# A re-planned instruction order, and GpSimd as a third engine for the attention's exponentials, in a four-layer transformer chain

## The chip, the cores and the metric

The kernel runs on one core of one Trainium2 chip. The metric is device time in microseconds of one execution. Times are medians of several runs; the profile is one further execution.

## The reference, cut to what matters

One sequence of 2048 tokens, width 1024, 32 heads of 32. Four residual layers alternate: A (linear attention with a learned softmax feature map), B (softmax attention), A, B, with the same weights each time they recur.

```python
def _A_ref(x, wqkv, w_phi, wo):            # q, k, v per head from x @ wqkv
    pq = jnp.einsum("bhsd,hdf->bhsf", q, w_phi)
    phi_q = jnp.concatenate([_softmax(pq), _softmax(-pq)], axis=-1)   # phi_k the same way
    kv = jnp.einsum("bhsf,bhsd->bhfd", phi_k, v)
    z  = jnp.einsum("bhsf->bhf", phi_k)
    o = einsum("bhqf,bhfd->bhqd", phi_q, kv) / (einsum("bhqf,bhf->bhq", phi_q, z)[..., None] + 1e-6)
    return o.transpose(0, 2, 1, 3).reshape(B, S, D) @ wo
def _B_ref(x, wqkv, wo):
    scores = jnp.einsum("bhqd,bhkd->bhqk", q, k) * (Dh ** -0.5)
    o = jnp.einsum("bhqk,bhkd->bhqd", _softmax(scores), v)
    return o.transpose(0, 2, 1, 3).reshape(B, S, D) @ wo
x = x + _A_ref(_layernorm(x), ...); x = x + _B_ref(_layernorm(x), ...)   # twice
```

Inputs and output are bf16.

## The kernel before

The kernel does not leave its order to a scheduler of the framework. It builds a list of operations, each with an engine, an expected duration, dependencies, buffers and a due time (`prio`), and a planner written in the file (`Sched`) places them in one fixed order for each engine. `LAT` (what passes from the end of an operation to the start of one on another engine), `act_us`, `dve_us`, `MM4` and the literals beside each operation are its expected durations; `WINDOW`, `QUOTA`, `AHEAD`, `NEAR`, `KL`, `PH` and the other capitals set how far ahead work may be taken, how many buffers a kind may hold and when side work is due. Once it is emitted, every engine runs its instructions strictly in that order and waits on semaphores.

Each of the two turns (`layer` 0 and 1) has an A part and a B part. In the A part TensorE products dominate: keys and values (`a_keys`), queries (`a_queries`), the output product (`a_out`); then `ln_rows` normalises each chunk of 512 tokens for B. `LN_DVE` says whether the row sums of that normalisation are taken on VectorE (`bn_stats`, L580) or on ScalarE (two passes with an accumulator, L586 and L588).

The B part is `attention`. Its work is 2048 units a layer: one unit is one head, 128 keys and 512 queries, a score tile of 128x512 in PSUM. The exponential of the scores goes to two engines:

- `group` takes up to three units (`WIDE`), scores them on TensorE side by side in rows of the array (L1148) into one of two buffers of three PSUM banks, and ScalarE exponentiates them in one instruction (L1208; 128x1536, or 128x1024 where a group has two units).
- A spare unit from some `AHEAD` units later may ride with a group in the fourth row, or as the third of a two-unit group. VectorE takes it out of PSUM (`convert`, L1290) as an integer whose bits hold the power of two, and later builds the exponential from the bits (`exp_dve`) by bit operations (L1102, L1105, or L1111, L1114) and products of two SBUF tensors (L1098). Up to two such units form a pair. In the second layer (`SPLIT`) the value is a sum of two bf16 parts, which costs TensorE one more product. `EACH` says whether the two units of a pair are computed singly.

The queries are scaled beforehand so that a score is the exponent of two times 2^23 (`ONE`).

The products with the values and with ones (L1337, both in one slot of the array) read the exponentials from SBUF, in the order of the units. In PSUM bank 7 fillers take their turn: projections of keys, values and queries, output products, in the first layer also the next A part's keys and values, and, where TensorE would have worked too little in the last microseconds, products that compute nothing (`idle`, `idle_acc`, L544 with onesD, L1573). GpSimd (POOL) sets a few buffers to zero and casts reciprocals (L779); it does nothing in the second attention. All DMAs are issued on SP's queue.

Of the kernel before, what the change touches and what calls it, by code (L numbers as in the profile page):

```python
# [46 lines left out]
LAT = {"PE": 0.25, "ACT": 0.2, "DVE": 0.1, "POOL": 0.2, "SP": 2.0, "AQ": 2.0}  # L47
# [13 lines left out]
class Sched:  # L61
# [134 lines left out]
    def run(self):  # L196
# [27 lines left out]
        while left:  # L224
# [107 lines left out]
WINDOW = 80.0  # L332
SOON = {"slabk": 24.0, "wo": 16.0, "w2": 4.0}
RESERVE = 12 * 1024
LONG = {"kT", "v", "slab", "slabk", "xn", "xn1", "kvacc", "kvm", "zm", "wnat"}
MODEST = {"slabk", "xn1", "e1", "vp1", "pkf", "wo", "bo"}
QUOTA = {"pk": 3, "pv": 2, "kv": 1, "mm": 5, "cmp": 2, "bc": 4, "num": 1, "wt": 4, "wx": 2, "fil": 4,
         "e": 6, "vp": 6, "e1": 4, "vp1": 4, "E": 8, "q2": 2, "kt": 4, "w2": 5, "oT": 26, "T": 4, "den": 2,
         "eq": 8, "ns": 4, "cw": 6, "hl": 6, "oc": 2, "slab": 7, "slabk": 3, "fin": 4,
         "rs": 8, "pkf": 1, "cden": 2, "part": 8, "w2r": 1,  # L340
         "wo": 1, "st": 4, "xo": 8, "bn": 4, "xs": 1, "xy": 4, "xx": 1, "E1": 7}
CORE = {"E", "E1", "T", "den", "cden", "oT"}
E_SIZE = 3 * 1024
HOLES = 2
# [10 lines left out]
EACH = (False, False)  # L355
LAG = 8
KL = (19, 32)
KS = (3, 5.5)
VS = (5.0, 7.0)
WQ_AFTER = 2  # L360
BY_DVE = 2
LR = 18
LAG_X = 4
LN_DVE = (True, True)
LN_PE = (3, 3)
WO = 6
KD = 7
HALF = (False, True)
VH = 3.0
QL = (11, 12)  # L370
AW = 23
OUT_AT = (230, 248, 268)
GO = 2.6
BO = 295
PT = 2.0
QB = 13
PH = (1, 22, 44)
LA = 9
AHEAD_AT = 5
P0 = (133, 167, 240)  # L380
GAPS = (1.5, 1.25, 1.75)
PK = (152, 192, 262)
STEP = 2.5
AWAY = (-2, 12)
MIX = (lambda i: 5, lambda i: 2)
LOAD = (4.0, 2.5)
AHEAD = (36, 34)
SLACK = 10.0
NEAR = (26, 18)
LEAD = 3.0  # L390
MOST = (lambda i: 0 if i < 1 else 7, lambda i: 0 if i < 1 else 6 if i < 6 else 40)
# [6 lines left out]
def dve_us(n):  # L398
    return n / 960 + 0.15
# [5 lines left out]
BACKLOG = 1.0  # L405
KV_MM = 0.042
# [3 lines left out]
def kernel(  # L410
# [49 lines left out]
    zz = const.tile([P, 16], F32, tag="zz")  # L460

# [3 lines left out]
    nc.vector.memset(eps[:], EPS_LN)  # L465
    make_identity(nc, ident[:])
# [65 lines left out]
    def dma(prio, fn, deps=(), bufs=(), q="SP", kb=256, issue=0.55, bulk=False):  # L532
        o = op(q, issue, fn, deps, bufs, prio, lat=2.0 + kb / 200.0)
        o.size, o.bulk = 256 if kb == 600 else kb, bulk
        return o
# [11 lines left out]
    MM4 = 0.225  # L547
# [534 lines left out]
    def exp_dve(pair, prio, each):  # L1082
# [6 lines left out]
        for lo, hi in [(k, k + 1) for k in range(n)] if each else [(0, n)]:  # L1089
# [4 lines left out]
            def ts(fn, deps, bufs):  # L1094
                return sch.later("DVE", w * 512 / 1920 + 0.15, fn, deps, bufs, prio)

            def stt(out_, in0, scalar, in1, dep, bufs):
                return sch.later("DVE", dve_us(w * 512), lambda: nc.vector.scalar_tensor_tensor(  # L1098
                    out=out_(), in0=in0(), scalar=scalar, in1=in1(), op0=ALU.add, op1=ALU.mult), [dep], bufs, prio)
            got = done[-1:] + pair["got"][lo:hi]  # L1100
            if pair["split"]:
                m = ts(lambda y_v=y_v, x_v=x_v: nc.vector.tensor_scalar(  # L1102
                    out=x_v().bitcast(I32), in0=y_v().bitcast(I32), scalar1=0x007FFFFF, scalar2=0x3F000000,
                    op0=ALU.bitwise_and, op1=ALU.bitwise_or), got, [y_b, x_b])
                a = ts(lambda y_v=y_v, e2_v=e2_v: nc.vector.tensor_scalar(  # L1105
                    out=e2_v().bitcast(U16), in0=high(y_v()), scalar1=0x7F80, scalar2=EXP2S_D,
                    op0=ALU.bitwise_and, op1=ALU.bitwise_or), [m], [y_b, e_b])
                h = stt(x_v, x_v, EXP2S_B, x_v, a, [x_b])
                done.append(stt(e_v, x_v, EXP2S_C, y_v, h, [x_b, y_b, e_b]))
                continue  # L1110
            m = ts(lambda y_v=y_v, x_v=x_v: nc.vector.tensor_scalar(  # L1111
                out=x_v().bitcast(I32), in0=y_v().bitcast(I32), scalar1=0x007FFFFF, scalar2=0x3F800000,
                op0=ALU.bitwise_and, op1=ALU.bitwise_or), got, [y_b, x_b])
# [5 lines left out]
            done.append(stt(e_v, x_v, EXP2_C, y_v, h, [x_b, y_b, e_b]))  # L1119
        return done  # L1120

    def attention(base, kT, vT, q_of, gate, most, mix, turns, pos, split, ahead, near, load, each):
# [7 lines left out]
        av_of, e_of, taken = {}, {}, set()  # L1130
# [22 lines left out]
        def holds(u):  # L1153
            return (kT[u[1]][0], q_of[(u[0], u[1])][0])
# [11 lines left out]
        def group(make):  # L1166
# [38 lines left out]
            so = make("PE", 0.24, sfn, sum((needs(u) for u in grp), []), [s_b], prio - 2, "r", n >= 2, [s_b])  # L1205
# [47 lines left out]

        def spare(rows, turn, more):

            pair = state["pair"]
# [26 lines left out]
        def convert(so, u, s_b, s_v, turn):  # L1283

            pair = state["pair"]
# [4 lines left out]
            pair["got"].append(sch.later("DVE", dve_us(512), lambda: nc.vector.tensor_scalar(  # L1290
                out=y_v().bitcast(I32)[:, k, :], in0=s_v(), scalar1=(EXP2S_OFF if split else EXP2_OFF) * ONE, scalar2=0.0,
                op0=ALU.add, op1=ALU.max), [so], [s_b, y_b], prio_of(u) - LEAD, None, True))
            state["turn"][turn] = state["turn"].get(turn, 0) + 1
            if k:
                close(pair)
# [16 lines left out]
        if True:  # L1312
            for qc, g in turns:
                T = []
                end = (qc, g) == turns[-1]
                for pp in range(2):
                    a_b, a_v = ps("acc", [(6,)])
                    last = None
                    for d in range(8):
                        prio = base + 10 * pos[(qc, g)] + 5 * pp + 0.5 * d  # L1320
                        for u in range(2):
# [22 lines left out]
                            last = op("PE", 0.225, fn, flat([last, v_done[(kc % 4, g % 4 // 2)]]),  # L1344
# [264 lines left out]
```

## Time and profile before

| | |
|---|---|
| median of 3 runs | 2275.22 us (2273.76 to 2275.47) |
| profiled execution, its own time | 2273.35 us |
| its span in the trace | 2271.6 us |
| mean granted TensorE clock | 0.997 |
| busy in the span: TensorE, ScalarE, VectorE, GpSimd | 2173.2, 1970.6, 1789.0, 27.0 us |

First attention about 330 to 1220 us, second about 1436 to 2260 us. In a row of the profile stand the line, the engine (PE is TensorE, ACT ScalarE, DVE VectorE, POOL GpSimd), the operation, output and input with their shapes, the count, busy time, the mean of one in ns, and after the second bar the engine's idle time just before, with what ended it. Means of instructions that overlap their neighbours on ScalarE and VectorE are longer than the distance from one start to the next.

### The profile page before, as it was taken

The numbers are of one execution on the slowest core, as the hardware profiler recorded it, in microseconds if no ns is written. First come the engines' busy times: TensorE is split into PE (matmuls) and PEld (weight loads), VectorE is DVE, ScalarE is ACT, GpSimd is POOL, SyncE is SP. The second block draws the span as 40 slices with busy tenths as digits, with TensorE's granted clock in tenths as the row PEclk, the third lists the DMA queues.
The fourth block names the chain that finished last, engine by engine and source line by source line (L and its number), as shares of the span: only waits on it lengthen the run. The fifth ranks groups of instructions, "written<-read, shape, count | busy, mean of one in ns | idle before, by whom it ended". The sixth has DMA issues, their size and how long they took to land.

```text
span 2271.6 us, 64125 instructions
## 1 busy us (share of the span) xinstructions
PE 2173.2 (96%) x27713; PEld 828.4 (36%) x27772; DVE 1789.0 (79%) x2645; ACT 1970.6 (87%) x1892; POOL 27.0 (1%) x78
## 2 busy tenths in 40 slices
PE   8999999999999999999998999999999999999998
PEld 5543443333333333333333444433333333333333
DVE  8867645876588978988896687276799999999897
ACT  6546449999999999999996544899999999999998
POOL 1000000000000000000000000000000000000000
PEclk9999999999999999999999999999999999999999
DMA  6711221111222424214424013201111111121111
GB/s 206 174 60 35 74 60 28 45 43 45 63 72 85 121 63 114 67 51 123 142 88 147 2 38 93 44 25 32 45 34 41 37 42 37 35 67 48 53 38 34
DMA packets 235188, 150.50 MB, mean 66 GB/s; under 512 B 131608, under 2 KB 211480, under 8 KB 234904
## 3 DMA queue, kind: packets, MB, share of 16 engines
q1 hardware_dynamic: 234904, 146.40, 23.5%
q8 instruction: 217, 3.56, 0.7%
q14 instruction: 67, 0.55, 0.1%
HBM read 81.59 MB, written 27.77 MB: 48 GB/s over the span
## 4 chain that ended last, share of the span: by engine, by line
PE 43%; ACT 42%; issue 10%; DVE 3%; DMA 2%; SPq 0%; ACTq 0%; DVEq 0%; another core or an unknown queue 0%
ACT arena L1208 40%; PE psum L540 18%; PE psum L544 8%; PE psum L1337 6%; PE psum L1148 6%; PE psum L931 1%; ACT arena L761 1%; PE psum L796 1%; DMA arena<-in_A_wqkv_dram 1%; DVE work L1290 1%; DVE work L1098 0%; PE psum L876 0%; DMA arena<-arena 0%; PE psum L942 0%; PE psum L685 0%
## 5 line engine op out<-in xcount | busy, mean ns | idle before, releaser
L1208 ACT ACTIVATE arena<-psum 128x1536 bf16<-128x1536 f32 (+1 forms) x1323 | 1681.0, 1539 | 15.2 <-PE psum L1148 10.1
L1337 PE MATMUL psum<-arena 128*32 128x512 bf16 x4324 | 663.9, 383 | 3.2 <-issue 2.0
L1337 PE MATMUL psum<-arena,ones_bf 128*32 128x512 bf16 x4324 | 664.5, 383 | 0.7 <-issue 0.7
L544 PE MATMUL psum<-arena 128*32 128x512 bf16 (+1 forms) x8768 | 604.1, 376 | 4.4 <-DVE arena L774 1.8
L1148 PE MATMUL psum<-arena 32*128 32x512 bf16 x4096 | 520.2, 382 | 60.5 <-ACT arena L1208 56.1
L540 PE MATMUL psum<-arena 128*128 128x512 bf16 (+1 forms) x1976 | 443.0, 373 | 11.2 <-DVE arena L1374 3.8
L1148 PEld LDWEIGHTS <-arena 32*128 32x128 bf16 x4096 | 171.4, 91 | 595.7 <-issue 589.6
L1290 DVE TENSOR_SCALAR work<-psum 128x512 int32<-128x512 f32 x371 | 254.7, 687 | 117.6 <-PE psum L1148 110.5
L1098 DVE SCALAR_TENSOR_TENSOR work<-work 128x1024 f32<-128x1024 f32 (+1 forms) x314 | 321.7, 1025 | 4.3
L544 PEld LDWEIGHTS <-arena 128*32 128x32 bf16 x8768 | 194.4, 95 | 241.5 <-issue 137.0
L540 PEld LDWEIGHTS <-arena 128*128 128x128 bf16 x2032 | 192.3, 98 | 232.2 <-issue 22.9
L1337 PEld LDWEIGHTS <-arena 128*32 128x32 bf16 x4324 | 188.2, 95 | 241.1 <-issue 160.5
L1098 DVE SCALAR_TENSOR_TENSOR arena<-work 128x1024 bf16<-128x1024 f32 (+1 forms) x215 | 229.4, 1067 | 2.8
L1337 PEld LDWEIGHTS <-ones_bf 128*32 128x32 bf16 x4324 | 187.1, 95 | 27.1 <-issue 2.5
L994 DVE CAST arena<-psum 128x512 bf16<-128x512 f32 (+1 forms) x104 | 67.2, 646 | 84.5 <-PE psum L544 83.9
L761 ACT ACTIVATE arena<-psum 128x512 bf16<-128x512 f32 x80 | 43.6, 594 | 75.3 <-PE psum L540 70.6
L893 ACT ACTIVATE arena<-psum 128x512 bf16<-128x512 f32 x128 | 70.6, 599 | 37.8 <-PE psum L540 26.7
L765 DVE TENSOR_REDUCE arena<-arena 128x32 f32<-128x1024 bf16 x64 | 77.8, 1215 | 23.9 <-ACT arena L761 23.2
L1353 DVE COPY arena<-psum 128x512 f32<-128x512 f32 x126 | 86.2, 684 | 12.0 <-PE psum L1337 11.6
L935 ACT COPY arena<-psum 128x512 f32<-128x512 f32 x64 | 37.2, 582 | 58.1 <-PE psum L931 52.0
L774 DVE TENSOR_TENSOR arena<-psum,arena 128x1024 bf16<-128x1024 f32 x64 | 77.4, 1210 | 6.4 <-PE psum L544 2.3
L1102 DVE TENSOR_SCALAR work<-work 128x1024 int32<-128x1024 int32 (+1 forms) x116 | 78.7, 678 | 2.4
(98 smaller groups left out, 1225.9 us busy)
## 6 DMA issues: line engine op xcount, KB each, us to landing
arena<-rd SPq DMA_DIRECT2D x62, 256.0 KB
arena<-in_B_wqkv_dram SPq DMA_DIRECT2D x51, 256.0 KB
xa<-arena SPq DMA_DIRECT2D x48, 256.0 KB
arena<-in_A_wqkv_dram SPq DMA_DIRECT2D x40, 256.0 KB
arena<-in_B_wo_dram SPq DMA_DIRECT2D x40, 256.0 KB
arena<-arena SPq DMA_DIRECT2D x256, 32.0 KB
arena<-wd_k SPq DMA_DIRECT2D x32, 256.0 KB
arena<-arena SPq DMA_DIRECT2D x62, 128.0 KB
```

Of the source, the lines that this page charges most:

```text
L540: nc.tensor.matmul(out_, lhsT=lhsT, rhs=rhs, start=start, stop=stop, skip_group_check=True)
L544: nc.tensor.matmul(out_[ks, :], lhsT=lhsT[:, ks], rhs=rhs, start=start, stop=stop, tile_position=(0, 32 * k), skip_group_check=True)
L765: red = op("DVE", dve_us(1024), lambda ev=ev, sv=sv: nc.vector.reduce_sum(out=sv(), in_=ev().rearrange("p s (h d) -> p (s h) d", d=DH), ax ...
L774: ml = op("DVE", dve_us(1024), lambda vpv=vpv, wv_=wv_, sv=sv: nc.vector.tensor_tensor(out=wv_()[:, :, :, 0:DH], in0=vpv().rearrange("p (h ...
L893: ex = [op("ACT", act_us(512), lambda s=s, pv=pv, ev=ev: nc.scalar.activation(out=ev()[:, s, :], in_=pv(), func=ACT.Exp, scale=(1.0, -1.0) ...
L1098: return sch.later("DVE", dve_us(w * 512), lambda: nc.vector.scalar_tensor_tensor(out=out_(), in0=in0(), scalar=scalar, in1=in1(), op0=ALU ...
L1102: m = ts(lambda y_v=y_v, x_v=x_v: nc.vector.tensor_scalar(out=x_v().bitcast(I32), in0=y_v().bitcast(I32), scalar1=0x007FFFFF, scalar2=0x3F ...
L1148: nc.tensor.matmul(out=out_, lhsT=kT[g][1]()[r, pp, d * P:(d + 1) * P], rhs=q_of[(qc, g)][1]()[r, (pp + j // 2) % 2, :], start=True, stop= ...
L1208: ex = make("ACT", act_us(w * C512), lambda: nc.scalar.activation(out=e_v()[:, 0:w * C512], in_=s_v()[:, 0:w * C512], func=ACT.Exp, scale= ...
L1290: pair["got"].append(sch.later("DVE", dve_us(512), lambda: nc.vector.tensor_scalar(out=y_v().bitcast(I32)[:, k, :], in0=s_v(), scalar1=(EX ...
L1337: nc.tensor.matmul(out=a_v()[col:col + 32, :], lhsT=v_v()[:, kc % 4, o:o + DH] if what == 0 else ones_bf[:], rhs=ev()[:, x * C512:(x + 1) ...
L1353: cp = op("DVE", dve_us(512), lambda t_v=t_v, a_v=a_v: nc.vector.tensor_copy(out=t_v(), in_=a_v()), [last], [a_b, t_b], prio - 4)
```

## The change

The planner's expected durations and nearly all of its settings are replaced, so that the whole order differs. One new path is added: a unit may be taken by GpSimd. `spare`, which looks for the unit that rides with a group, first asks `spare_pool`: if GpSimd has at most 4 us queued by the planner's count, it takes a unit 90 to 97 units ahead, with an fp32 buffer `gy` and a bf16 buffer `E2`. VectorE takes the unit out of PSUM as fp32, divided by 2^23, and GpSimd raises 2 to it in four instructions of 128 columns, for which the planner books 5 us each. The value products read `E2` like any other exponential.

```diff
-LAT = {"PE": 0.25, "ACT": 0.2, "DVE": 0.1, ...}
+LAT = {"PE": 0.28, "ACT": 0.07, "DVE": 0.17, ...}
-WINDOW = 80.0
+WINDOW = 85.0
-EACH = (False, False)
-LAG = 8
-KL = (19, 32)
+EACH = (True, False)
+LAG = 6
+KL = (20, 26)
-LN_DVE = (True, True)
+LN_DVE = (False, True)
-PH = (1, 22, 44)
+PH = (-3, 22, 46)
-AHEAD = (36, 34)
+AHEAD = (34, 34)
-NEAR = (26, 18)
+NEAR = (30, 10)
-MIX = (lambda i: 5, lambda i: 2)
-LOAD = (4.0, 2.5)
+MIX = (lambda i: 1, lambda i: 0)
+LOAD = (3.5, 1.0)
...
 def dve_us(n):
-    return n / 960 + 0.15
+    return n / 960 + 0.07
+GP = 20.0
+GP_AHEAD = 90
+GP_NEXT = 4.0
+GP_CUT = 4
...
+    nc.vector.memset(two[:], 2.0)
...
-    MM4 = 0.225
+    MM4 = 0.2165
...
+        def spare_pool(rows, more):
+            if state["at"] + GP_AHEAD + 8 > len(units) or sch.load("POOL") > GP_NEXT:
+                return None
+            u = next((u for u in units[state["at"] + GP_AHEAD:state["at"] + GP_AHEAD + 8]
+                      if u[4] in rows and u not in taken
+                      and all(d.done == 2 for d in needs(u))), None)
+            if u is None:
+                return None
+            y_b, y_v = sb("gy", C512, dt=F32)
+            e_b, e_v = sb("E2", C512)
...
+            by_pool[u] = (y_b, y_v, e_b, e_v)
+            taken.add(u)
+            return u
         def spare(rows, turn, more):
+            u = spare_pool(rows, more)
+            if u is not None:
+                return u
             pair = state["pair"]
...
         def convert(so, u, s_b, s_v, turn):
+            if u in by_pool:
+                y_b, y_v, e_b, e_v = by_pool[u]
+                so.bufs += holds(u)
+                cv = sch.later("DVE", dve_us(512) + 0.13, lambda: nc.vector.tensor_scalar(
+                    out=y_v(), in0=s_v(), scalar1=1.0 / ONE, scalar2=None, op0=ALU.mult), [so], [s_b, y_b],
+                    prio_of(u) - LEAD, None, True)
...
+                for h in range(GP_CUT):
+                    at = slice(h * C512 // GP_CUT, (h + 1) * C512 // GP_CUT)
+                    ex = sch.later("POOL", GP / GP_CUT, lambda at=at: nc.gpsimd.tensor_tensor(
+                        out=e_v()[:, at], in0=two[:, 0:1].to_broadcast([P, C512 // GP_CUT]), in1=y_v()[:, at],
+                        op=ALU.pow), [cv], [y_b, e_b], prio_of(u) - LEAD)
+                used(u, ex, e_b, e_v, 0)
+                return
```

Lines of the changed kernel that the prediction names: L1104 for L1098 (two-tensor steps), L1108 and L1111 for L1102 and L1105, L1117 and L1120 for L1111 and L1114, L1214 for L1208 (ScalarE's exponential), L1321 (taking out for GpSimd), L1328 (the power), L1338 for L1290, L1385 for L1337. Counted in the two programs' orders, GpSimd takes 67 units, 30 in the first attention and 37 in the second.

More of the change, by code (lines that the diff above doesn't have):

```diff
@@ L44, in __init__ @@
         self.size, self.bulk = 0, False
-LAT = {"PE": 0.25, "ACT": 0.2, "DVE": 0.1, "POOL": 0.2, "SP": 2.0, "AQ": 2.0}
+LAT = {"PE": 0.28, "ACT": 0.07, "DVE": 0.17, "POOL": 0.2, "SP": 2.0, "AQ": 2.0}
 SWITCH = 0.1
@@ L460 @@
     zz = const.tile([P, 16], F32, tag="zz")
+    two = const.tile([P, 1], F32, tag="two")
     nc.vector.memset(onesD[:], 1.0 / D)
@@ L1204, in sfn @@
                     score(u, xv())
-            so = make("PE", 0.24, sfn, sum((needs(u) for u in grp), []), [s_b], prio - 2, "r", n >= 2, [s_b])
+            so = make("PE", 0.2165, sfn, sum((needs(u) for u in grp), []), [s_b], prio - 2, "r", n >= 2, [s_b])
             for u in grp:
@@ L1289, in convert @@
             pair["units"].append(u)
[L1290 removed]
+            pair["got"].append(sch.later("DVE", dve_us(512) + 0.13, lambda: nc.vector.tensor_scalar(
                 out=y_v().bitcast(I32)[:, k, :], in0=s_v(), scalar1=(EXP2S_OFF if split else EXP2_OFF) * ONE, scalar2=0.0,
```

93 lines of the change are left out of this document (52 added, 41 removed).

## Prediction

> **What bounds the kernel now.** I read the page's slices first, then its chain, then ScalarE's largest group with its shapes kept apart, then windows.
>
> ```profile
> ACT  6546449999999999999996544899999999999998
> PE 43%; ACT 42%; issue 10%; DVE 3%; DMA 2%; SPq 0%; ACTq 0%; DVEq 0%; another core or an unknown queue 0%
> ...
> L544 PE MATMUL psum<-xR,onesD 128*32 128x512 bf16 x888 | 69.6, 380 | 0.4 <-DVE work L1290 0.2
> L1573 PE MATMUL psum<-xR,zero 128*32 128x512 bf16 x400 | 34.0, 379 | 0.0
> ```
>
> In the slices ScalarE (ACT) is full twice: these are the two softmax attentions. TensorE shows nine tenths nearly everywhere, but 69.6 + 34.0 us of it are the last two rows, filler products that compute nothing and are put in only where TensorE would have been under-used. The chain alternates between ACT's exponential and the scores, because each exponential frees the PSUM banks that the next scores need. Which of the two paces it is told by ACT's idle time.
>
> ```profile
> L1208 ACT ACTIVATE arena<-psum 128x1536 bf16<-128x1536 f32 x1079 | 1518.7, 1615 | 15.2 <-PE psum L1148 10.1 <-PE psum L1337 4.9
> L1208 ACT ACTIVATE arena<-psum 128x1024 bf16<-128x1024 f32 x244 | 293.3, 1202 | 0.0
> 326.00:1226.00 900.00, 852.86 (x12530) 301.97 (x12528) 701.67 (x1034) 884.29 (x725) 10.04 (x25) 1.00 0.28 76
> 1226.00:1427.00 201.00, 193.74 (x1313) 88.30 (x1334) 145.97 (x254) 98.74 (x193) 2.59 (x8) 0.98 0.23 67
> 1427.00:2256.00 829.00, 802.00 (x11041) 282.29 (x11040) 692.13 (x942) 818.53 (x663) 0.00 (x0) 1.00 0.15 40
> ```
>
> The windows (length, then busy PE, weight load, DVE, ACT, POOL, each with its count, then the granted clock) are the first attention, the stretch between, and the second attention. ACT waited 15.2 us ahead of 1323 exponentials. So in both attentions time is what ACT has to do; VectorE (DVE) is at 78% and 83%, GpSimd (POOL) nearly free. In the 201 us between, TensorE is the bound.
>
> **Part 1: exponentials taken from ACT.** A unit is 512 columns. I need the step of one exponential from start to start; the rows' means overlap. Two stretches of 100 us without idle ACT give it:
>
> ```profile
> L1208 ACT ACTIVATE arena<-psum 128x1536 bf16<-128x1536 f32 x68 | 94.3, 1603 | 0.0
> L1208 ACT ACTIVATE arena<-psum 128x1024 bf16<-128x1024 f32 x11 | 13.2, 1196 | 0.0
> ...
> L1208 ACT ACTIVATE arena<-psum 128x1536 bf16<-128x1536 f32 x61 | 87.2, 1600 | 0.1
> L1208 ACT ACTIVATE arena<-psum 128x1024 bf16<-128x1024 f32 x21 | 24.4, 1164 | 0.0
> ...
> L1208 ACT ACTIVATE arena<-psum 128x1536 bf16<-128x1536 f32 (+1 forms) x1323 | 1681.0, 1539 | 15.2 <-PE psum L1148 10.1 <-PE psum L1337 4.9
> ```
>
> The first pair is 500 to 600 us, the second 1600 to 1700. Equal time for 68 wide and 11 narrow as for 61 and 21 makes the narrow form 0.7 of the wide. With that, 1079 wide and 244 narrow fill the group row's 1681.0 us at 1.345 and 0.941 us each. A count of one at a window's edge makes the share 0.64 to 0.78; with 0.78 the two gains below together are 13 us smaller.
>
> The two programs' instruction orders give the counts. First attention: 571 wide and 96 narrow become 507 and 168, so 1905 units become 1857; that is 858.3 us becoming 840.0, **-18.3 us**. Second: 508 and 148 become 469 and 196 (1820 to 1799 units), 822.5 becoming 815.2, **-7.3 us**. The gain is smaller than 69 units suggest because more exponentials are narrow. VectorE's own units go from 143 to 161 in the first attention and from 228 to 212 in the second; POOL gets 30 and 37.
>
> **Part 2: VectorE.** Its rows for window 326:1226, then for 1427:2256:
>
> ```profile
> L1098 DVE SCALAR_TENSOR_TENSOR work<-work 128x1024 f32<-128x1024 f32 x88 | 107.3, 1220 | 1.8
> L1290 DVE TENSOR_SCALAR work<-psum 128x512 int32<-128x512 f32 x143 | 98.1, 686 | 53.9 <-PE psum L1148 50.6 <-ACT arena L1208 2.5
> L1098 DVE SCALAR_TENSOR_TENSOR work<-work 128x512 f32<-128x512 f32 x110 | 75.6, 687 | 2.5
> L1098 DVE SCALAR_TENSOR_TENSOR arena<-work 128x1024 bf16<-128x1024 f32 x44 | 53.5, 1216 | 0.6
> L1098 DVE SCALAR_TENSOR_TENSOR arena<-work 128x512 bf16<-128x512 f32 x55 | 37.7, 685 | 1.2
> L1114 DVE TENSOR_SCALAR work<-work 128x1024 int32<-128x1024 int32 x44 | 30.3, 688 | 0.9
> L1111 DVE TENSOR_SCALAR work<-work 128x1024 int32<-128x1024 int32 x44 | 30.2, 686 | 1.0
> L1114 DVE TENSOR_SCALAR work<-work 128x512 int32<-128x512 int32 x55 | 23.2, 422 | 1.4
> L1111 DVE TENSOR_SCALAR work<-work 128x512 int32<-128x512 int32 x55 | 22.9, 417 | 0.4
> ...
> L1098 DVE SCALAR_TENSOR_TENSOR work<-work 128x1024 f32<-128x1024 f32 x112 | 136.1, 1215 | 0.0
> L1098 DVE SCALAR_TENSOR_TENSOR arena<-work 128x1024 bf16<-128x1024 f32 x112 | 135.5, 1210 | 0.9
> L1102 DVE TENSOR_SCALAR work<-work 128x1024 int32<-128x1024 int32 x112 | 77.1, 688 | 2.4
> L1105 DVE TENSOR_SCALAR arena<-work 128x1024 uint16<-128x1024 uint16 x112 | 76.5, 683 | 0.0
> ...
> 900.00:1000.00 100.00, 90.54 (x1493) 33.51 (x1493) 89.60 (x127) 98.82 (x89) 2.85 (x8) 1.00 0.27 79
> ```
>
> First attention, before: 380.7 us for the five-step exponential of 143 units, the sum of the eight rows other than L1290. EACH makes all 161 single: 161 x (2 x 0.687 + 0.685 + 0.417 + 0.422) = 466.6 us, +85.9. Taking 191 units out of PSUM instead of 143 is +48 x 0.686 = 32.9. So 701.7 becomes 820.5 us in a stage of about 882: 93%. Second: a pair costs (136.1 + 135.5 + 77.1 + 76.5) / 112 = 3.80 us; six pairs and four short singles fewer and 21 takings-out more give 692.1 - 31.5 + 14.4 = 675 of 827, 82%. VectorE stays the second engine, but its cover in the first attention shrinks from 198 to 62 us. Behind each taking-out in its queue stand the evacuations that TensorE waits for. Where it was at 89.6% (the last row), ACT still idled 1.18 us in 100; at 93% I take 2%, 17.6 us, against some 10 now (900 less 884.3, less the edges): **+8 us**, between 0 and 20.
>
> **Part 3: GpSimd.** 268 powers of 128x128, four for a unit, fp32 in, bf16 out. No row shows a power. The nearest rows are a cast and a fill:
>
> ```profile
> L779 POOL CAST arena<-arena 128x32 bf16<-128x32 f32 x64 | 21.3, 332 | 1238.1 <-PE psum L1148 694.1 <-DVE arena L768 410.4 <-PE psum L1337 49.1
> L836 POOL MEMSET arena<- 128x2048 bf16 x2 | 3.7, 1846 | 0.1
> ```
>
> From below, a piece takes 0.33 us, the time of a quarter of its columns; at the cast's rate it is 1.3 us. No row bounds it above. The planner books 5 us, 20 for a unit, and its order is spaced for that: 23 times two units follow within four exponentials, and then the second's last piece stands 5 to 10 exponentials, 6 to 13 us, ahead of its first reader on TensorE. Shorter powers cost nothing; longer ones than about 23 to 26 us a unit stall TensorE. I take the planner's 5 us as the least certain term, hidden by that lead: 0 us. The casts L779 wait for at most one piece; their readers stand behind VectorE's multiplication as before.
>
> **Part 4: the stages around.** Layer 0's second normalisation goes from VectorE to ACT, two passes and two accumulator reads in place of two statistics:
>
> ```profile
> L586 ACT ACTIVATE arena<-xR 128x1024 bf16<-128x1024 bf16 x8 | 8.4, 1051 | 0.0
> L586 ACT ACTIVATION_READ_ACCUMULATOR arena<-xR 128x1 f32 x8 | 1.6, 196 | 0.0
> L580 DVE BATCH_NORM_STATS2 arena<-xR 128x6 f32<-128x512 bf16 x112 | 71.7, 668 | 0.0
> L540 PE MATMUL psum<-arena 128*128 128x512 bf16 (+1 forms) x1976 | 443.0, 373 | 11.2 <-DVE arena L1374 3.8 <-issue 2.7 <-DMA arena<-in_A_wqkv_dram 1.3
> ```
>
> A tile costs 2 x (1.05 + 0.20) = 2.5 us of ACT in place of 2 x 0.67 of VectorE. Three of four chunks hide under TensorE's products, ACT being half free there by the slices; in the last one four tiles stand in line, 4 x 1.2 = 4.6 us more, of which I take **+3 us** as exposed, -2 to 8 with the new order of that stretch. Before the second attention 12 full and 56 half products of the last value chunk move behind its first scores: 40 x 443.0 / 1976 = 9.0 us less of TensorE ahead, some 1 us of other products more; ACT takes over about 5 us of their evacuations inside the attention: **-3 us**. New waits of DMA queues I cost at nothing: the transfers' numbers and sizes are the same.
>
> **The sum.** -18.3 - 7.3 + 8 + 3 - 3 = -17.6 us. The profiled execution's own time is 2273.35, which gives 2255.8; the median of the runs lies 1.87 above it: **2257 us**. Its own range is 2238 (no new idle, narrow form cheap, stages -5) to 2270.
>
> **Rival 1: POOL keeps VectorE out of SBUF.** The trace already shows this, in the first 5 us and at 905 us:
>
> ```profile
> 3.03 1.81 POOL L836 MEMSET arena<- 128x2048 bf16 x1
> ...
> 3.00 1.87 DVE L712 COPY rep<-J_bf 128x32 bf16<-128x32 bf16 x1 [1.94 <-POOL J_bf L709]
> 3.11 1.79 DVE L715 CAST fold<-ident 128x32 f32<-128x32 bf16 x1
> ...
> 905.61 0.57 POOL L779 CAST arena<-arena 128x32 bf16<-128x32 f32 x1 [27.02 <-DVE arena L768]
> ...
> 905.37 0.63 DVE L1111 TENSOR_SCALAR work<-work 128x1024 int32<-128x1024 int32 x1
> ```
>
> A 32-column copy took 1.87 us and ended with POOL's fill; the other way, a cast of 0.33 us took 0.57 beside a VectorE step. If a power holds VectorE so for its whole 5 us, then per piece VectorE does one step that needs the common way and the work up to the next. First attention: 161 x 5 exponential steps and 31 other two-tensor products, 836, so 0.98 us of its 820.5 us per piece; POOL's 120 pieces (600 us) carry 118 us, and 600 + 820.5 - 118 = 1302 us against 882. Second: 455 steps, 1.48 us a piece, 148 pieces: 740 + 675 - 219 = 1196 against 827. Together +789, **3046 us**. If only the double-rate steps (two of five, two of four) are held, 322 and 212 of them, the stages become 1114 and 944: +349, **2606 us**. If all are held but a piece takes 2 us, only the first attention grows, by 60: 2317. The point from which it decides: 120 x (p - 0.98) over 62, a piece of 1.5 us. Against it: a fill writes without pause while a power computes most of its time, and reading may be done early; no row tells.
>
> The Trainium skill says the same in "SBUF — State Buffer", Who interferes with whom: GpSimd and VectorE share a port pair under an exclusive lock; its table of terms adds that it is held for the full instruction and blocks the loser fully. By that rule the 3046 us hold for 5 us pieces; the fill and the copy above agree with it, and a power is shown by no run yet.
>
> The Trainium skill's "GPSIMD Engine Reference", Elementwise — side-by-side cycle accounting, has 2.6 cycles an element for a two-input addition; as an estimate that is 0.28 us for 128 columns at the 1.2 GHz it names, and the sum would stay as it is.
>
> **Rival 2: the power is longer than booked.** With 30 us a unit, each of 23 pairs comes 20 us later than planned and about 10 us late for TensorE: +230, 2490 us.
>
> **Rival 3: the change brings nothing**, since VectorE at 93% hands gain back as idle ACT (+20 in place of +8, the stages' +8 in place of +3, and no shift of the second attention): -25.6 + 20 + 8 = +2.4, so 2278, between 2270 and 2290.
>
> **How the numbers follow.** The forecast 0.47; rival 1 in full 0.16, in part (2300 to 2610) 0.20; rival 2 0.09; rival 3 0.08. For the forecast speaks that its terms rest on ACT, whose bound is plain in the rows; for rival 1 the copy of 1.87 us; neither shows the power itself. What a measurement can tell from no change is 0.2%, 4.6 us. Faster: 0.45 of the forecast and 0.01 of rival 3, 0.46. Within 0.2%: 0.02 and 0.04, 0.06. Slower: 0.16 + 0.20 + 0.09 + 0.03 = 0.48. So both signs are about as likely, and the forecast is the likeliest single case. The range runs from 2238 to 2620, which leaves out rival 1 in full and little else.
>
> **What would show it.** Right: the exponential's group at about 1655 us with under 35 us of idle, VectorE's steps L1117 and L1120 still at 0.42 us, and L1338 at 0.69, POOL busy where the scores run. Rival 1: those steps, or L1104, at some microseconds, VectorE above 95% with ACT waiting for TensorE and TensorE for VectorE. Rival 2: waits of TensorE's L1385 for POOL L1328, and pieces beyond 6 us. Rival 3: idle ahead of the exponential above 40 us with all steps unchanged. The forecast is wrong if ACT is no longer full in both attentions.

## The result, and the profile after

The changed kernel takes **6372.57 us** (6372.37 to 6372.97, four runs) against 2275.34 before (2273.76 to 2279.25, four runs): a ratio of 2.8007, with a 95% interval of 2.7962 to 2.8051. The forecast of 2257 and the whole range up to 2620 were far too low, and the forecast's direction was wrong.

From the page of the profile after, three engines and the granted clock in the slices, then the three rows that matter:

```profile
DVE  8522338221322232223631112231221221212232
ACT  4732339231322232223543122231322221312232
POOL 0089882999999999997069999999999999999996
PEclk9976669665666666566986666665666665666666
...
L1328 POOL TENSOR_TENSOR arena<-two,arena 128x128 bf16<-128x128 f32 x268 | 5556.0, 20756 | 532.2 <-DVE arena L1321 306.7
L1214 ACT ACTIVATE arena<-psum 128x1536 bf16<-128x1536 f32 (+1 forms) x1340 | 1681.4, 1369 | 3914.6 <-PE psum L1154 2426.1
L1385 PE MATMUL psum<-arena 128*32 128x512 bf16 x4308 | 724.8, 414 | 1738.9 <-POOL arena L1328 1146.8
```

ScalarE, full in both attentions before, is at two to three tenths, and GpSimd (POOL) is full. One power of 128 columns took 20.756 us, not the 5 that the planner booked. A unit's four cost 83 us, and all 268 come to 5556 of the span's 6371 us. TensorE's value products (L1385) waited 1146.8 us for powers directly; ScalarE stood idle 3914.6 us ahead of its exponentials (15.2 before): 2426.1 until scores came, which stand on TensorE behind those products, and 788.4 until a power ended. An exponential reads no power; both write into the common buffer `arena`, so these are waits for room in it, as far as the profile tells. The granted clock fell to 0.677 of full speed on average, with TensorE busy 37% of the span; it does not set the time, since GpSimd is full beside it.

What VectorE did beside a power is shown by the timeline of after (start, length, engine, line, and in brackets the idle time before with its releaser), with GpSimd's row first, and by two of VectorE's groups with their shapes kept apart:

```profile
1963.86 103.46 POOL L1328 TENSOR_TENSOR arena<-two,arena 128x128 bf16<-128x128 f32 x5
...
2009.28 0.42 DVE L1117 TENSOR_SCALAR work<-work 128x512 int32<-128x512 int32 x1
2009.73 0.43 DVE L1120 TENSOR_SCALAR work<-work 128x512 int32<-128x512 int32 x1
2010.19 1.42 DVE L1104 SCALAR_TENSOR_TENSOR work<-work 128x512 f32<-128x512 f32 x2
2067.36 0.69 DVE L763 COPY arena<-psum 128x512 f32<-128x512 f32 x1 [55.75 <-POOL arena L1328]
```

```profile
L1338 DVE TENSOR_SCALAR work<-psum 128x512 int32<-128x512 f32 x373 | 255.9, 686 | 1107.2 <-PE psum L1154 1103.2 <-issue 2.4
L1104 DVE SCALAR_TENSOR_TENSOR work<-work 128x512 f32<-128x512 f32 x322 | 221.9, 689 | 7.8
```

Five powers follow each other without a gap from 1963.9 to 2067.3 us. Within them VectorE does its bit steps in 0.42 us and its products in 0.7, as before the change; then it stands for 55.75 us, by the profile until a power is finished. The copy that comes then (L763) reads PSUM and writes into `arena`; it needs no power's result, so what it waited for seems to be room that the power still held. VectorE was kept waiting by a dependency of the program; its steps were not slowed. Over the whole run its two-input steps of 512 columns kept their 689 ns (687 before).

### The profile page after: what moved, and what is told of

Its sections match the earlier page's. It is cut to its first block, busy times and chain, and to the rows that moved or that the text cites. A ratio compares the mean times of both kernels' runs of the same rounds, so it can differ in the third digit from the quotient of the medians.

```text
span 6371.2 us, 65312 instructions
## 1 busy us (share of the span) xinstructions
PE 2352.9 (37%) x27956; PEld 835.4 (13%) x27956; DVE 1863.9 (29%) x2969; ACT 2007.0 (32%) x1973; POOL 5578.0 (88%) x346
## 5 line engine op out<-in xcount | busy, mean ns | idle before, releaser
L1328 POOL TENSOR_TENSOR arena<-two,arena 128x128 bf16<-128x128 f32 x268 | 5556.0, 20756 | 532.2 <-DVE arena L1321 306.7
L1214 ACT ACTIVATE arena<-psum 128x1536 bf16<-128x1536 f32 (+1 forms) x1340 | 1681.4, 1369 | 3914.6 <-PE psum L1154 2426.1
L1385 PE MATMUL psum<-arena 128*32 128x512 bf16 x4308 | 724.8, 414 | 1738.9 <-POOL arena L1328 1146.8
L1154 PE MATMUL psum<-arena 32*128 32x512 bf16 x4096 | 569.0, 413 | 1497.0 <-ACT arena L1214 779.0
L550 PE MATMUL psum<-arena 128*32 128x512 bf16 (+1 forms) x8768 | 666.1, 405 | 499.9 <-DVE arena L763 190.9
L1385 PE MATMUL psum<-arena,ones_bf 128*32 128x512 bf16 x4308 | 725.0, 414 | 0.0
L1338 DVE TENSOR_SCALAR work<-psum 128x512 int32<-128x512 f32 x373 | 255.9, 686 | 1107.2 <-PE psum L1154 1103.2
L1385 PEld LDWEIGHTS <-ones_bf 128*32 128x32 bf16 x4308 | 190.8, 99 | 1771.5 <-issue 1753.2
L1104 DVE SCALAR_TENSOR_TENSOR work<-work 128x512 f32<-128x512 f32 (+1 forms) x428 | 351.0, 820 | 7.8
L550 PEld LDWEIGHTS <-arena 128*32 128x32 bf16 x8768 | 206.9, 100 | 1084.5 <-issue 912.1
L1104 DVE SCALAR_TENSOR_TENSOR arena<-work 128x512 bf16<-128x512 f32 (+1 forms) x267 | 241.3, 904 | 255.6 <-POOL arena L1328 251.3
L1385 PEld LDWEIGHTS <-arena 128*32 128x32 bf16 x4308 | 194.2, 98 | 564.9 <-issue 494.7
L1321 DVE TENSOR_SCALAR arena<-psum 128x512 f32<-128x512 f32 x67 | 46.0, 686 | 583.9 <-POOL arena L1328 496.6
L785 POOL CAST arena<-arena 128x32 bf16<-128x32 f32 x64 | 20.2, 321 | 211.0 <-DVE arena L774 185.0
L1012 DVE TENSOR_SCALAR arena<-psum 128x512 bf16<-128x512 f32 x40 | 27.4, 686 | 286.5 <-PE psum L550 169.5
L550 PE MATMUL psum<-xR,onesD 128*32 128x512 bf16 x1024 | 87.5, 409 | 57.1 <-DVE work L1338 56.0
```

The costliest lines, as they stand in the source:

```text
L550: nc.tensor.matmul(out_[ks, :], lhsT=lhsT[:, ks], rhs=rhs, start=start, stop=stop, tile_position=(0, 32 * k), skip_group_check=True)
L1104: return sch.later("DVE", dve_us(w * 512) + us, lambda: nc.vector.scalar_tensor_tensor(out=out_(), in0=in0(), scalar=scalar, in1=in1(), op ...
L1154: nc.tensor.matmul(out=out_, lhsT=kT[g][1]()[r, pp, d * P:(d + 1) * P], rhs=q_of[(qc, g)][1]()[r, (pp + j // 2) % 2, :], start=True, stop= ...
L1214: ex = make("ACT", act_us(w * C512), lambda: nc.scalar.activation(out=e_v()[:, 0:w * C512], in_=s_v()[:, 0:w * C512], func=ACT.Exp, scale= ...
L1328: ex = sch.later("POOL", GP / GP_CUT, lambda at=at: nc.gpsimd.tensor_tensor(out=e_v()[:, at], in0=two[:, 0:1].to_broadcast([P, C512 // GP_ ...
L1338: pair["got"].append(sch.later("DVE", dve_us(512) + 0.13, lambda: nc.vector.tensor_scalar(out=y_v().bitcast(I32)[:, k, :], in0=s_v(), scal ...
```

## The experiments

**What a power costs, and why.** Theories: the planner's price is wrong (rival 2), or VectorE is held (rival 1). Four edits of the changed kernel. The first closes GpSimd's path and keeps every other setting of the new plan, so that ScalarE and VectorE take its units; the second makes one instruction of 512 columns out of four; the third multiplies where the power was raised, while order, buffers and waits stay; the fourth raises 2 to zero only.

```
order alone:        GP_NEXT = 4.0             ->  GP_NEXT = -1.0
one instruction:    GP_CUT = 4                ->  GP_CUT = 1
product for power:  op=ALU.pow                ->  op=ALU.mult
power of zero:      scalar1=1.0 / ONE (L1322) ->  scalar1=0.0
```

> The changed kernel with its path to GpSimd closed (no unit is taken by it; VectorE takes 402 units, ScalarE 3694). Theory (the power's duration is the whole cause): the new order alone loses nothing; ScalarE has 31 units fewer than before but 315 narrow groups in place of 244, so 1021 x 1.345 + 315 x 0.941 = 1670 us against 1681, about 11 us less, and the time is 2255 to 2275. Rival (the new order is itself at fault, durations and settings unfit for the chip): above 2400, with ScalarE idle ahead of its exponentials for hundreds of us though GpSimd does nothing.

> The power in one instruction of 512 columns for each unit in place of four of 128 (GP_CUT 1), with the planner's 20 us for it as before. If the power's time goes by columns (162 ns each in the changed kernel), one instruction takes 83 us, and the time stays at about 6300. If it is a cost of each instruction, whatever its columns, one takes about 21 us, a unit keeps the planner's booking, and the time is near the forecast: 2245 to 2300.

> The power replaced by a product of the same two operands (2 times the scaled score), so that 67 units enter the attention with wrong weights; instructions, shapes, order and waits are the same. Theory (duration alone): pieces of 0.3 to 1.5 us, GpSimd never late, 2245 to 2265. Rival (GpSimd's two-operand instructions hold VectorE out of SBUF or wait for it, which long powers only hid): VectorE's steps of 0.42 and 0.69 us grow beside GpSimd's, by up to a piece each, and the time is above 2280.

> The scores of GpSimd's units are multiplied by 0 on the way out of PSUM, so that every power is 2 to the 0 and 67 units have weights of one. If the power's time depends on the numbers (large or fractional exponents), the pieces get clearly shorter than 20.7 us and the time falls in proportion; if it is the same code for every number, they stay at 20.7 us and the time at 6370.

The order alone took 2266.4 us, a ratio of 0.996 (0.9948 to 0.9972). With the product in the power's place, so that 67 units get no exponential, it was 2257.44, ratio 0.9915 (0.9901 to 0.9929): only the kind of operation differs from the changed kernel, and 4115 us are gone. One instruction a unit took 6327.14 (2.7793, 2.7761 to 2.7824), powers of zero 6372.8 in one run. GpSimd's group in the product's run (with its min/median/max in ns, first to last start), in the single instruction's and in the zeros':

```profile
L1328 POOL TENSOR_TENSOR arena<-two,arena 128x128 bf16<-128x128 f32 x268 | 144.4, 568 | 1567.9 <-DVE arena L1321 1010.7 <-DMA arena<-arena 278.7 <-issue 178.5
...
L1328 POOL TENSOR_TENSOR arena<-two,arena x268: 392/401/1415, 338.7 to 2171.8; 128x128 bf16<-128x128 f32 x134
```

```profile
L1328 POOL TENSOR_TENSOR arena<-two,arena 128x512 bf16<-128x512 f32 x67 | 5488.1, 81933 | 551.8 <-DVE arena L1321 506.5 <-DMA rd<-arena 20.6 <-issue 18.2
```

```profile
L1328 POOL TENSOR_TENSOR arena<-two,arena 128x128 bf16<-128x128 f32 x268 | 5555.5, 20754 | 532.5 <-DVE arena L1321 307.0 <-DMA arena<-arena 178.2 <-issue 28.8
```

So 512 columns in one go cost 81.9 us and in four 83.0: the price is some 159 ns a column and only 0.3 us an instruction, and exponents of zero cost the same. None of the four went against the theory that the power's duration is the whole cause.

**How much the order can bear.** In these three each piece raises only some columns to the power and multiplies the rest, which sets the price of a piece at will in an unchanged order.

```
for a0, a1, alu in ((lo, lo + 30, ALU.pow), (lo + 30, hi, ALU.mult)):     # of 128; then 48, then 24
    nc.gpsimd.tensor_tensor(out=e_v()[:, a0:a1], in0=two ..., in1=y_v()[:, a0:a1], op=alu)
```

> The changed kernel's order and waits, but of each piece of 128 columns only the first 30 are raised to a power and the other 98 get the plain product (so 98 of 128 columns of 67 units have wrong weights). At 162 ns a column and 0.3 to 0.4 us for the product a piece takes about 5.3 us and a unit 21, close to the planner's booking of 20. Theory (only the power's size was wrong): 2257 to 2270, as with the plain product. Rival (a power as such disturbs the other engines): clearly above 2270 though the unit is as long as booked.

> As the run with 30 columns, but 48 of 128 raised to a power (80 get the plain product): a piece takes about 8.1 us and a unit 32, beyond the 23 to 26 us that the order's lead was said to bear. Theory: each of 23 pairs comes 24 us later than planned with 6 to 13 us of lead, so some 14 us late: 23 x 14 = 330 us more if no lateness is shared, and at least GpSimd's own 67 x 32 = 2170 us in stages of 1710: 2500 to 2800. Rival (the lead is longer than counted): below 2350.

> The changed kernel's order, with 24 of each 128 columns raised to a power and the plain product in the other 104 (so those have wrong weights): 24 x 0.162 + 0.3 + 0.47 = 4.7 us a piece, 18.6 us a unit, just under the booked 20 (30 columns came to 23.0). Theory (the order bears exactly what it booked, since GpSimd stands at nine tenths in the second attention): 2255 to 2265, ScalarE idle below 25 us. Rival (a power, or GpSimd at work for 1250 us, disturbs the others in itself): above 2290, since 23.0 us a unit already cost 115 us.

GpSimd's powers with 24 and with 30 columns, each with the exponential's group of the same run:

```profile
L1328 POOL TENSOR_TENSOR arena<-two,arena 128x24 bf16<-128x24 f32 x268 | 1167.2, 4355 | 666.6 <-DVE arena L1321 375.3 <-DMA arena<-arena 200.6 <-issue 69.5
L1214 ACT ACTIVATE arena<-psum 128x1536 bf16<-128x1536 f32 (+1 forms) x1340 | 1656.9, 1410 | 15.5 <-PE psum L1154 11.0 <-PE psum L1387 2.4 <-PE psum L550 0.4
```

```profile
L1328 POOL TENSOR_TENSOR arena<-two,arena 128x30 bf16<-128x30 f32 x268 | 1416.1, 5284 | 570.4 <-DVE arena L1321 325.4 <-DMA arena<-arena 194.0 <-issue 47.1
L1214 ACT ACTIVATE arena<-psum 128x1536 bf16<-128x1536 f32 (+1 forms) x1340 | 1665.0, 1391 | 122.3 <-PE psum L1154 79.0 <-POOL arena L1328 31.0 <-PE psum L1387 8.2
```

With the product on the other columns a unit cost 19.5, 23.0 and 34.1 us. The times were 2257.65 (0.9922, 0.9909 to 0.9936), 2372.99 (1.0427, 1.0413 to 1.0442) and 3089.26 in one run. The second and third are misses of what I expected: I had kept the prediction's limit of 23 to 26 us. No power as such disturbs the others: with 24 columns GpSimd computed powers for 1167.2 us and nothing was lost. The limit lies between 19.5 and 23.0 us. GpSimd's row in the second attention of the product's run tells where, and the exponential's rows by attention of the run with 30 columns tell what lies beyond it:

```profile
L1328 POOL TENSOR_TENSOR arena<-two,arena x148: 392/401/1415, 1433.0 to 2171.8; 128x128 bf16<-128x128 f32 x148
```

```profile
L1214 ACT ACTIVATE arena<-psum x675: 1003/1460/1776, 330.8 to 1233.6; 128x1536 bf16<-128x1536 f32 x123, 128x1024 bf16<-128x1024 f32 x46
L1214 ACT ACTIVATE arena<-psum x665: 1018/1458/1749, 1442.9 to 2359.6; 128x1536 bf16<-128x1536 f32 x115, 128x1024 bf16<-128x1024 f32 x52
```

The 148 pieces start between 1433.0 and 2171.8 us; that is 739 us, and 37 units by the booked 20 are 740. The plan books GpSimd there without a gap, so a late unit hands its lateness to the next, and each microsecond above 20 adds up to 37 us. At 23.0 that is 111 us at most. From first to last start the second attention took 916.7 us, 86.5 more than with products (the table near the end has those). The first took 902.8, 29.7 more, although 30 units of 20 us fill only 600 of its 873: they are spread unevenly over it (with 24 columns GpSimd's busy share there goes from none to nine tenths). So 111 lies close to the 115 measured partly by luck. From 34.1 to 83.0 us a unit the time rose by 67 us for each microsecond: there every unit of both attentions counts in full. GpSimd's timeline of the changed kernel shows it for the second attention, 148 powers with one gap of 10.63 us:

```profile
3242.01 662.80 POOL L1328 TENSOR_TENSOR arena<-two,arena 128x128 bf16<-128x128 f32 x32 [178.16 <-DMA arena<-arena]
3915.44 2406.53 POOL L1328 TENSOR_TENSOR arena<-two,arena 128x128 bf16<-128x128 f32 x116 [10.63 <-issue]
```

Counted from the booked 20, the sum is 67 x (83 - 20) = 4221 us, and 4115 were measured.

**Is there a cheaper power?** In these VectorE hands over 1 + t, and GpSimd makes the exponential from it with eight products and one scaling, nine short steps on each piece. First with the booking unchanged, then with all 512 columns in one instruction, booked 12 us (109 units).

```
VectorE:  scalar1=e_scale / 2**SQ, scalar2=1.0, op0=ALU.mult, op1=ALU.add          # SQ = 7
GpSimd:   y = y*y;  y = 0.5*y + 0.5;  then SQ times y = y*y, the last one into e_v()
second kernel also:  GP = 20.0 -> 12.0,  GP_CUT = 4 -> 1
```

> The changed kernel's order, but the exponential on GpSimd comes from products: VectorE hands over 1 + t, with t the score's exponent over 128; GpSimd squares, halves with a half added (1 + t + t*t/2), and squares seven times, nine steps of 128 columns for a piece. By the plain product's 0.4 us that is 3.6 us a piece and 14.5 us a unit, inside the booking. Theory (a unit shorter than booked costs nothing): 2255 to 2262. Rival (GpSimd's two-tensor steps and VectorE's hold each other up when there are 2400 of them): VectorE's steps grow by more than 0.05 us in the mean and the time is above 2270.

> The same products, in instructions of 512 columns and booked at 12 us a unit: the planner gives GpSimd 109 units, VectorE 356, ScalarE 3630 (960 wide, 375 narrow: 960 x 1.345 + 375 x 0.941 = 1644 us against 1655 in the changed order). Theory (ScalarE paces): about 10 us less than with 67 units, 2242 to 2255. Rival (contention with VectorE, or steps of 512 longer than 1.3 us so that the booking is again too short): above 2270.

Both missed: 2402.94 us (1.056, 1.0544 to 1.0576) and 2609.36 (1.1462, 1.1446 to 1.1478). VectorE's groups by form, two of the run with the order alone, then two of the second kernel here with GpSimd's own step:

```profile
L1104 DVE SCALAR_TENSOR_TENSOR work<-work 128x1024 f32<-128x1024 f32 x116 | 141.1, 1217 | 0.0
L1111 DVE TENSOR_SCALAR arena<-work 128x1024 uint16<-128x1024 uint16 x116 | 79.4, 685 | 0.0
```

```profile
L1332 POOL TENSOR_TENSOR arena<-arena 128x512 f32<-128x512 f32 x654 | 858.3, 1312 | 51.8
L1105 DVE SCALAR_TENSOR_TENSOR work<-work 128x1024 f32<-128x1024 f32 x101 | 175.0, 1732 | 0.0
...
L1112 DVE TENSOR_SCALAR arena<-work 128x1024 uint16<-128x1024 uint16 x101 | 123.0, 1218 | 0.0
```

The same VectorE steps went from 1.217 to 1.732 us and from 0.685 to 1.218 (L1105 and L1112 are L1104 and L1111, moved by a line). With pieces of 128 columns they were 1.346 and 0.821. GpSimd's own step is hardly a measure of it: there it had a mean of 0.561 us and a median of 0.399, against 0.568 and 0.401 for the lone product above. That GpSimd's products are what lengthens VectorE's steps is plain within the second kernel, where GpSimd stands still up to 1817 us and then works (GpSimd's row, then VectorE's bit steps before and after):

```profile
1817.17 1.88 POOL L1329 TENSOR_TENSOR arena<-arena 128x512 f32<-128x512 f32 x1 [22.18 <-DVE arena L1322]
...
1811.86 0.69 DVE L1109 TENSOR_SCALAR work<-work 128x1024 int32<-128x1024 int32 x1
1812.47 0.68 DVE L1112 TENSOR_SCALAR arena<-work 128x1024 uint16<-128x1024 uint16 x1
...
1833.38 1.52 DVE L1109 TENSOR_SCALAR work<-work 128x1024 int32<-128x1024 int32 x1
1834.83 1.52 DVE L1112 TENSOR_SCALAR arena<-work 128x1024 uint16<-128x1024 uint16 x1
```

Here, then, is rival 1: VectorE's steps grow when GpSimd runs short products in close succession. It isn't the whole of the first miss. There GpSimd's steps with the gaps between them come to 22.6 us a unit, above the booked 20, as in the run with 30 columns. In the second kernel they come to 12.1, next to the 12 booked, so VectorE's longer steps are the likeliest cause left there; no run takes them away in that order.

Three more of this kind book 25 us, 110 units ahead: in both attentions; in the second only (`or not split`); in the second only and never with a second unit of GpSimd's in hand (`or sch.live.get("gy", 0)`).

> The products in place of the power (nine steps a piece, 128 columns), booked at 25 us a unit, what they took beside VectorE in the first trial, and taken 110 units ahead: 50 units on GpSimd, 387 on VectorE, 3659 on ScalarE (991 wide and 342 narrow: 1655 us of ScalarE). Theory (a right booking is all that is missing): 2255 to 2266. Rival (contention: VectorE at 93% in the first attention cannot bear steps 7 to 20% longer): above 2280, with VectorE's two-tensor steps at 0.73 us and more.

> The same, only in the second attention, where VectorE has room: 30 units on GpSimd, 389 on VectorE (1002 wide, 335 narrow: 1663 us of ScalarE). Theory: 2258 to 2268, slightly below the new order alone (2266). Rival (contention): above 2275.

> The products (nine steps a piece of 128 columns, booked at 25 us a unit, 110 units ahead), in the second attention and one unit at a time: 24 units. Two causes are open for the 24 us that 30 units cost there against the new order alone: units taken in pairs, or VectorE's steps made longer by GpSimd's (L1112 at 0.83 us in place of 0.69). If pairs: 2260 to 2270. If contention: 2275 to 2290, since GpSimd then still runs some 550 us beside VectorE.

They took 2326.72 us (1.0224, 1.021 to 1.0238), 2290.02 (1.0061, 1.0049 to 1.0074) and 2280.77 (1.0024, 1.0014 to 1.0033), with 50, 30 and 24 units. The first two missed and fell where their rival, contention, had put them; in the first a unit took 24.0 us with its gaps, less than the 25 booked, so its loss isn't the booking's. The third lies where contention put it and not where pairs did. In it, VectorE's two steps are still at 1.321 and 0.796 us in the mean. Fewer units came ever closer to the kernel before, but none passed the order alone.

**The real power, booked at its price.** GP = 83 and 220 units ahead: in the second attention only (4 units); in both, one unit at a time (7 units); the same with pieces of 32 columns, queries prepared 14 places earlier and one more buffer for them (12 units).

```
GP = 20.0 -> 82.8 or 83.0;  GP_AHEAD = 90 -> 220
... or not split                      # the first;   second and third:  or sch.live.get("gy", 0)
GP_CUT = 4 -> 16;  QL = (16, 19) -> (30, 33);  "q2": 4 -> 5       # the third alone
```

> The power itself, booked at the 82.8 us that it takes, taken 220 units ahead and only in the second attention: the order then holds 4 units on GpSimd (399 on VectorE, 1017 wide and 321 narrow on ScalarE: 1670 us). Theory (the booking was the whole fault): no loss against the new order alone, 2262 to 2272, and nothing to gain either. Rival: above 2280.

> The power booked at 83 us a unit and taken 220 units ahead, and now only one unit at a time: while a unit's fp32 buffer lives, no other is taken. 7 units on GpSimd, 398 on VectorE (1010 wide and 330 narrow on ScalarE: 1669 us). Theory (with 4 units the order booked at 82.8 us lost 144 us because they were taken in pairs, 167 us on end against a lead of some 95): no loss against the new order alone, 2260 to 2272. Rival (a power so long disturbs the order whatever is booked): above 2290.

> The same in pieces of 32 columns (5.3 us each), with queries made 14 units of due time earlier and one more buffer for them, so that more units are ready so far ahead: 12 units on GpSimd, 402 on VectorE (1006 wide and 332 narrow: 1665 us). Theory: 2256 to 2270, as far as the earlier queries cost nothing. Rival: above 2290, with TensorE waiting for GpSimd's pieces.

All three missed: 2410.31 us (1.0595, 1.058 to 1.0609), 2292.16 (1.0071, 1.0059 to 1.0083), 2318.35 (1.0188, 1.0175 to 1.0201). The first one's GpSimd timeline and, from its waits (in total, times, longest), TensorE's for powers:

```profile
1981.68 167.43 POOL L1328 TENSOR_TENSOR arena<-two,arena 128x128 bf16<-128x128 f32 x8 [721.31 <-DVE arena L1321]
2154.64 167.81 POOL L1328 TENSOR_TENSOR arena<-two,arena 128x128 bf16<-128x128 f32 x8 [5.54 <-DVE arena L1321]
...
PE psum L1385 <- POOL arena L1328: 102.2, 2, 59.7
```

Eight pieces in a row are two units: the question `sch.load("POOL") > GP_NEXT` sees nothing of a unit whose score VectorE hasn't yet taken out, so a second one is taken at once and its powers come late: TensorE waited 102.2 us in two waits. By the code, the prediction's 23 pairs have the same source.

One unit at a time removes that: the exponential's group of that run (7 units) idled 18.1 us. The time went elsewhere. Its rows for L1214 (min/median/max, then first to last start) in each attention, and TensorE's output products L550 from the last exponential of the first attention to the first step of the normalisation, in it and in the order alone:

```profile
L1214 ACT ACTIVATE arena<-psum x675: 610/1472/1722, 330.7 to 1213.4; 128x1536 bf16<-128x1536 f32 x133, 128x1024 bf16<-128x1024 f32 x36
...
L1214 ACT ACTIVATE arena<-psum x666: 1017/1469/1748, 1439.4 to 2276.5; 128x1536 bf16<-128x1536 f32 x120, 128x1024 bf16<-128x1024 f32 x47
```

```profile
L550 PE MATMUL psum<-arena 128*32 128x512 bf16 x168 | 12.9, 443 | 6.3 <-DVE arena L1068 3.9 <-DMA arena<-in_B_wo_dram 2.5
```

```profile
L550 PE MATMUL psum<-arena 128*32 128x512 bf16 x24 | 1.5, 380 | 0.0
```

From the last exponential of the first attention to the first of the second it is 226.0 us, against 208.6 in the order alone: 17.4 of the 25.8 us lost. In place of 24 output products 168 were left over at the edge. The planner, given these prices, put them there; which of its choices does it was not tried. In the run with 12 units ScalarE idled 51.2 us and GpSimd again ran 180 us without a gap twice, yet TensorE's value products waited only 5.8 us for it; as three settings were changed at once, I leave its cause open.

## Why the prediction was wrong, and where it was right

**The step that failed is part 3's "0 us".** It took "the planner's 5 us" a piece, and said itself that no row bounds a power above. Measured: 20.7 us, some 160 ns a column. Having no upper row, I priced rival 2 at 30 us a unit and gave it 0.09; the point from which it decides was in my own numbers and I did not work it out. 37 units of 20 us are 740 of 827 us in the second attention: a price about an eighth above the booked one fills the stage, and from 34.1 us on each microsecond of price cost 67. Rival 2's mechanism was the right one, its sign (waits of L1385 for L1328, pieces beyond 6 us) is in the profile, and its size was off by some 3900 us. The remark that the casts wait for at most one piece failed with the price: TensorE waited up to 62.7 us for one (L802 for L785), about three powers.

**The limit of "23 to 26 us a unit" failed too.** I measured one pair's lead against its reader and forgot that lateness adds up on an engine booked without a gap: 19.5 us a unit gave the forecast's time, 23.0 cost 115 us more. It was the smaller fault: at the booked 20 us GpSimd is hidden, as the run with 19.5 shows.

**Rival 1 was wrong for the power and right for products.** During a 20.7-us power VectorE's steps kept 0.42 and 0.69 us. The Trainium skill's "SBUF — State Buffer", Who interferes with whom, by which the lock is held for the full instruction, does not hold for this operation by these rows. For products in close succession VectorE's 0.685-us step took 1.218 in the mean, which agrees with the rule that the two engines share a port. The fill of 1.81 us and the copy behind it thus look like a row of the second kind, not of the power's, though no run here tells why a power is different; I had given the rival 0.36.

**The rest of the sum stands, once the price is what was booked.** With pieces of 24 powers, 2257.65 us; with products, 2257.44; forecast 2257. The exponential's group came to 1656.9 and 1657.2 us (forecast 1655) with 15.5 and 16.2 of idle (under 35). Window rows of the run with products, for the stages of part 2 (length, then busy PE, weight load, DVE, ACT, POOL):

```profile
326.00:1226.00 900.00, 861.02 (x12666) 298.81 (x12666) 813.63 (x1408) 872.86 (x747) 70.65 (x145) 0.99 0.29 82
1427.00:2256.00 829.00, 800.26 (x11131) 275.63 (x11124) 686.26 (x935) 811.15 (x665) 81.50 (x148) 1.00 0.15 40
```

VectorE's 813.6 and 686.3 us stand against 820.5 and 675 forecast, and even so ScalarE hardly waited: the +8 us of new idle did not come. Yet the agreement of the total is better than that of its parts, as the first and last starts show (rows of the exponential, by attention: before, the order alone, the product):

```profile
L1208 ACT ACTIVATE arena<-psum x667: 1018/1615/1863, 330.4 to 1217.5; 128x1536 bf16<-128x1536 f32 x139, 128x1024 bf16<-128x1024 f32 x28
L1208 ACT ACTIVATE arena<-psum x656: 1018/1565/1803, 1435.8 to 2259.2; 128x1536 bf16<-128x1536 f32 x121, 128x1024 bf16<-128x1024 f32 x43
```

```profile
L1214 ACT ACTIVATE arena<-psum x674: 1005/1474/1722, 330.8 to 1210.8; 128x1536 bf16<-128x1536 f32 x131, 128x1024 bf16<-128x1024 f32 x38
L1214 ACT ACTIVATE arena<-psum x663: 658/1473/1822, 1419.4 to 2253.4; 128x1536 bf16<-128x1536 f32 x118, 128x1024 bf16<-128x1024 f32 x48
```

```profile
L1214 ACT ACTIVATE arena<-psum x675: 1005/1469/1772, 331.9 to 1205.0; 128x1536 bf16<-128x1536 f32 x123, 128x1024 bf16<-128x1024 f32 x46
L1214 ACT ACTIVATE arena<-psum x665: 1017/1471/1732, 1414.6 to 2244.8; 128x1536 bf16<-128x1536 f32 x115, 128x1024 bf16<-128x1024 f32 x52
```

| from start to start, us | before | order alone | product |
|---|---|---|---|
| first attention | 887.1 | 880.0 | 873.1 |
| between the attentions | 218.3 | 208.6 | 209.6 |
| second attention | 823.4 | 834.0 | 830.2 |

The first attention lost 14.0 us (forecast -18.3 + 8 = -10.3), and the new start cost 1.5 of the 3 us of part 4. The stretch between became 9 us shorter, as part 4 has it, but the second attention became 6.8 longer where it was to lose 7.3 (10.6 longer with the order alone). The products that part 4 moved into it may be what lengthens it; no run here moves them alone. Together these two stages brought 1.9 us of the 10.3 forecast. In the profiled executions the whole gain was 2273.35 - 2258.41 = 14.9 us where 17.6 were forecast; by the medians it was 17.9. The errors of the terms, 3.7 and 1.5 us too cautious and 8.4 too hopeful, nearly cancel: that 2257.44 falls on 2257 is luck, while the kind of bound, ScalarE full in both attentions, was right. About half of the gain, 9 us, is the order's; GpSimd's 67 units bring the other 9, if they cost GpSimd no more than 20 us each and do not lengthen VectorE's steps. Neither operation tried does both, and the fastest version measured that computes the whole reference is the order alone, 2266.4 us.

## What to carry to other kernels

Measure an operation that the profile doesn't show before a plan is built on its price; where that can't be done, compare the engine's booked total with the length of the stage, for that margin, and not the lead of a single piece, says how wrong the price may be. To split a loss between an operation's cost and the order around it, put a cheap operation with the same operands in its place: here that one word returned 4115 us and the forecast's time. What an engine does to its neighbour depends on the operation too, so the row of a fill told nothing of the power here.

## What the runs showed of the hardware

- A power of two fp32 operands on GpSimd takes some 159 ns a column of 128 partitions and 0.3 us an instruction (20.7 us for 128 columns, 81.9 for 512), with exponents of zero as with the scores; a product of the same operands has a median of 0.40 us for 128 columns, some fifty times less.
- A power leaves VectorE's steps as they are (two inputs of 512 columns 689 ns, 687 before); GpSimd's products of 512 columns in close succession (1.31 us each) lengthened VectorE's steps of 1024 columns by 42% (two inputs) and 78% (bit steps).
- With TensorE busy 37% of the span, its granted clock averaged 0.677, against 0.997 before.
